# Output sums by rows of 16-token stride, without the scratch tensor for the convolution's results

## The chip, the cores and the metric

One core of one Trainium2 chip. The metric is the device time of one execution in microseconds (us), as the median of several runs. A profile is one further execution, and has a time of its own.

## The reference, cut to what matters

The kernel computes, for 2048 tokens of width 512, a gated mix of two branches:

```python
x = A_x
g = sigmoid((x * gate_w).sum(-1, keepdims=True))
a = A_ref(x, wq, wk, wv, wo, beta)   # attention
b = B_ref(x, A, B, C, log_dt, Dskip) # state-space convolution
return g * a + (1 - g) * b
```

Branch A has 32 heads of width 16 and four segments of 512 tokens. Within a segment it is causal softmax attention; each head mixes to it, by a gate of its own, a linear-attention memory of the earlier segments (elu + 1 features, M and z summed up over the segments). The heads' outputs go through `wo`. Branch B is a causal convolution of each of the 512 channels with a kernel of length 2048, `K[d, l] = Re sum_n C B dt exp(dt A l)`, plus the skip `u * Dskip`.

## The kernel before, in words

The program is a graph of 1846 steps that `build_graph` writes down (`S.op`, `S.dma`, `S.evac`); a step is one or several instructions on one engine. Which step runs when is not in the graph: the text `ORDER` (line 366) lists the numbers of all steps, and each engine executes its steps in this sequence. Behind a number, the slashes give the buffer slots that the step takes; `a` or `v` picks ACT or DVE for a copy out of PSUM that either could make. `Sched.emit` sets a semaphore wait wherever a step needs another engine's result or a buffer's last reader. An engine takes its steps strictly in this order, so a step that waits holds up those behind it on its engine. Nearly all DMAs are issued by SP, one after the other.

What the steps do:

- **x transposed** (`do_xT`, line 731) puts x into SBUF as channels by tokens (`xTT`); `gate_tokens` (903) computes the token gate g per segment, 16 matmuls of one column, an exponential on ACT (915) and small DVE operations (914 to 920). Line 918 makes 1 - g, for the output sums.
- **Attention.** For each of 4 segments s and 4 groups of 8 heads: `project` (q, k), `seg_tokens` (v), `seg_state` (the memory), `scores` (1019) in five tiles A0, B0, C, A1, B1, each with matmuls into four PSUM banks, one exponential over 2048 columns on ACT (line 1080, 80 in all), a mask (1092) and the product with V (matmuls of 17 columns); then the normalization (1052, 1053, 1055). `ophase` (1111) adds the memory and transposes the result (step oT) to channels by tokens (`oTT`).
- **Tables** (`tables`, 1148) build the convolution kernel's factors on DVE (lines 1177 to 1217).
- **Convolution** by a transform in two levels. `x_level1` (872) reads x in rows of 16-token stride (partition j holds tokens 16 j, 16 j + 1, ...) and writes the first level to the DRAM scratch `scr_Z`. `tail` (1257) runs twice, for channels 0 to 255 (half a) and 256 to 511 (half b), 16 steps each: load constants (CT, CD) and the first level (Zx) from `scr_Z`, transform (X, with two SBUF-to-SBUF moves that exchange the partition halves, also called X), the kernel's transform (K), the product (Y, line 1309), back (V, moved into V2). At its end, eight steps `fir` finish the inverse: four matmuls of 256 columns each over V2, and four of 128 columns that add the skip, whose stationary operand is `xTT` with a stride of 16 tokens, `[[16, 128]]`. A fir result has partition j holding token 16 j + b: rows of 16-token stride.
- **Bounce.** The output sums want 128 consecutive tokens on the partitions. So fir's results (`cv`) go to the scratch tensor `scr_C` by 8 DMAs and come back by 8 more (Cl) as `CTT`, tokens in sequence.
- **Output sums** (`final`, 1352; called for s and tb): for 128 consecutive tokens four matmuls of 512 columns (one for each head group) give attention times `wo` in PSUM; DVE adds (1 - g) times `CTT` (1371) and a DMA stores 128 rows to the output. For s = 3 the fourth matmul is a step of its own, behind the last transposed output. Six buffers `ou` take the results.

All matmuls are issued by the helper in line 699; copies out of PSUM by `evac` (226 on ACT, 227 on DVE); DMAs by `S.dma` (222). PSUM has 8 banks; a score tile takes four of them, always the same.

The profiles' lines name the steps by line; the names here (oT3.3 is the transposed output of segment 3, head group 3; sc, mk, pv, nrm are the tile's scores, mask, V product and normalization; Xb7 is transform step 7 of half b) are the program's tags.

## Time and profile before

| what | us |
|---|---|
| median of 3 runs | 309.71 (309.55 to 310.97) |
| the profiled execution | 306.98 |
| its span, first to last instruction | 305.2 |
| PE busy, DVE busy, ACT busy | 262.4, 269.4, 260.1 |
| time at the last exponential's start | 282.48 |
| last output sum's end | 298.9 |

A profile row gives the source line, the engine, the operation and its operands; "x16" counts instructions. "busy" is the time in which at least one of a group's instructions ran, "mean ns" that of one. In a row of the windows stand, after the stretch and its length, the busy time and count of PE, PEld (TensorE's weight loads), DVE, ACT and POOL, then the granted clock, the DMA engines' share and GB/s. In the chain of waits and in the timeline the first two numbers are start and length; a bracket tells how long the engine was idle before and what ended that. PE's busy time is longer than what its matmuls need: they are pipelined, and each has its full latency in the record.

### The profile page before, as it was taken

What the parts mean: (1) busy time and instruction counts of PE and PEld (TensorE: products, weight loads), DVE (VectorE), ACT (ScalarE), POOL (GpSimd) and SP (SyncE); (2) the same over time, 40 slices, a digit from 0 to 9 for tenths busy, and PEclk for the clock granted to TensorE, in tenths of its full rate; (3) what the DMA queues carried; (4) which work ended last, traced back from release to release, by engine and by line L of the source; (5) the groups of instructions that cost most, each with busy time, mean ns of one, the idle gap of its engine ahead of it and who ended that gap; (6) DMA issues with size and microseconds to landing.
All of it is one profiled execution on the core that took longest, in us unless ns stands there. A gap on an engine that the chain in (4) does not pass through costs nothing.

```text
span 305.2 us, 10349 instructions
## 1 busy us (share of the span) xinstructions
PE 262.4 (86%) x4360; PEld 184.8 (61%) x4395; DVE 269.4 (88%) x653; ACT 260.1 (85%) x304; POOL 7.9 (3%) x18
## 2 busy tenths in 40 slices
PE   6586678887888899999999899899899899998990
PEld 5242445653556576677766667687676777886540
DVE  2999999989999999989998987899889769989781
ACT  2999999999999999969999879899699798988200
POOL 8000000000000000000000000000000000000000
PEclk9999999999999999999999999999999999999998
DMA  7994662262234554636766466677767876367752
GB/s 172 244 232 100 146 178 77 78 100 66 85 93 110 156 163 121 193 88 176 212 176 184 145 191 196 181 220 237 232 190 218 248 227 174 97 179 217 194 174 70
DMA packets 60738, 49.89 MB, mean 163 GB/s; under 512 B 22594, under 2 KB 56019, under 8 KB 60691
## 3 DMA queue, kind: packets, MB, share of 16 engines
q1 hardware_dynamic: 59728, 48.84, 57.7%
q8 instruction: 35, 0.57, 0.9%
q0 software_dynamic: 288, 0.21, 0.5%
q10 hardware_dynamic: 674, 0.16, 0.2%
q14 instruction: 13, 0.10, 0.1%
HBM read 28.88 MB, written 8.39 MB: 122 GB/s over the span
## 4 chain that ended last, share of the span: by engine, by line
PE 32%; ACT 30%; DVE 18%; DMA 10%; issue 6%; SPq 2%; DVEq 0%; ACTq 0%
PE psum L699 31%; ACT sb L1080 17%; ACT sb L226 10%; DMA sb<-sb 4%; DMA sb<-in_A_wv_dram 3%; DVE sb L1180 3%; DVE sb L1177 2%; DVE sb L1371 2%; DVE sb L1184 2%; DVE sb L227 2%; SPq L222 2%; ACT sb L820 1%; DMA sb<-scr_Z 1%; DVE sb L1309 1%; DMA out_dram<-sb 1%
## 5 line engine op out<-in xcount | busy, mean ns | idle before, releaser
L699 PE MATMUL psum<-sb 128*128 128x17 bf16 (+12 forms) x4242 | 254.1, 224 | 29.8 <-ACT sb L1080 12.1
L699 PEld LDWEIGHTS psum<-sb 128*128 128x128 bf16 (+5 forms) x4277 | 176.5, 98 | 103.7 <-ACT sb L1080 22.2
L1080 ACT ACTIVATE sb<-psum 128x2048 bf16<-128x2048 f32 x80 | 152.2, 1902 | 9.2 <-PE psum L699 8.4
L226 ACT ACTIVATE sb<-psum 128x512 bf16<-128x512 f32 (+2 forms) x159 | 93.2, 650 | 17.4 <-PE psum L699 16.6
L227 DVE CAST sb<-psum 128x512 bf16<-128x512 f32 x62 | 42.5, 692 | 7.6 <-PE psum L699 7.4
L1309 DVE TENSOR_TENSOR sb<-sb 128x1024 bf16<-128x1024 bf16 x32 | 22.0, 686 | 5.1 <-DMA sb<-sb 4.7
L1092 DVE TENSOR_TENSOR sb<-sb 128x1024 bf16<-128x1024 bf16 (+1 forms) x40 | 22.8, 578 | 3.0 <-ACT sb L1080 2.8
L1177 DVE TENSOR_TENSOR sb<-sb 128x512 bf16<-128x512 bf16 (+4 forms) x44 | 24.5, 565 | 0.4
L1184 DVE TENSOR_TENSOR sb<-sb 128x512 bf16<-128x512 bf16 (+4 forms) x44 | 24.2, 554 | 0.5
L1180 DVE TENSOR_TENSOR sb<-sb 128x512 bf16<-128x512 bf16 (+4 forms) x44 | 24.5, 564 | 0.2
L1055 DVE TENSOR_TENSOR sb<-psum,sb 128x256 bf16<-128x256 f32 x32 | 13.5, 422 | 0.5
L820 ACT ACTIVATE sb<-sb 128x512 f32<-128x512 f32 x18 | 11.8, 655 | 0.2 <-DVE sb L802 0.2
L1371 DVE SCALAR_TENSOR_TENSOR sb<-sb,psum 128x512 bf16<-128x512 bf16 x16 | 10.7, 736 | 1.1 <-DMA out_dram<-sb 1.1
L1217 DVE TENSOR_TENSOR sb<-sb 128x2048 bf16<-128x2048 bf16 x8 | 9.6, 1224 | 0.1
L1212 DVE TENSOR_TENSOR sb<-sb 128x4096 bf16<-128x4096 bf16 x4 | 9.1, 2285 | 0.0
L1052 DVE RECIPROCAL sb<-psum 128x16 f32<-128x16 f32 x32 | 8.1, 254 | 1.1 <-PE psum L699 0.8
L1132 DVE TENSOR_TENSOR sb<-psum,sb 128x512 bf16<-128x512 f32 x12 | 8.3, 689 | 0.3
L1009 ACT ACTIVATE sb<-sb 128x512 bf16<-128x512 bf16 x12 | 7.8, 652 | 0.0
L821 DVE TENSOR_TENSOR sb<-sb 128x256 f32<-128x256 f32 x18 | 7.6, 420 | 0.2
L227 DVE COPY sb<-psum 128x1024 bf16<-128x1024 bf16 x4 | 2.8, 688 | 5.5 <-PE psum L765 5.0
L822 DVE SCALAR_TENSOR_TENSOR sb<-sb 128x256 f32<-128x256 f32 x18 | 7.6, 420 | 0.1
L958 ACT ACTIVATE sb<-psum 128x512 bf16<-128x512 bf16 x12 | 7.5, 627 | 0.1
(75 smaller groups left out, 115.8 us busy)
## 6 DMA issues: line engine op xcount, KB each, us to landing
sb<-c_DNM SPq DMA_DIRECT2D x32, 320.0 KB, 4.0
sb<-c_DNM SPq DMA_DIRECT2D x32, 192.0 KB, 3.4
sb<-sb SPq DMA_DIRECT2D x84, 64.0 KB, 2.9
scr_Z<-sb SPq DMA_DIRECT2D x16, 256.0 KB, 2.4
sb<-scr_Z SPq DMA_DIRECT2D x32, 128.0 KB, 2.8
sb<-sb SPq DMA_DIRECT2D x32, 128.0 KB
sb<-in_A_x_dram SPq DMA_DIRECT2D x5, 512.0 KB, 5.7
scr_C<-sb SPq DMA_DIRECT2D x8, 256.0 KB, 3.1
```

The source lines that it names most:

```text
L226: fa = lambda e: e.activation(dst(), src(), ACT.Copy)
L227: fd = lambda e: e.tensor_copy(dst(), src())
L699: mm = lambda e, o_, l, r_, st, sp, **kw: e.matmul(o_, lhsT=l, rhs=r_, start=st, stop=sp, skip_group_check=True, **kw)
L820: op("ACT", ("As", 512), lambda e, sq=sq, Z=Z: e.activation(ap(sq, n=512), ap(Z, n=512), ACT.Square), r=[Z], w=[sq], key=PW[h] + PWS * k)
L1055: op("DVE", ("V1", 256), lambda e: e.tensor_tensor(ap(o1, gi * 16, [[128, 4], [32, 4], [1, 16]]), ap(T, dims=[[68, 4], [17, 4], [1, 16]]), ...
L1080: o = op("ACT", ("Ax", 2048), lambda e, P=P, pT=pT: e.activation(ap(pT, n=2048), ap(P, n=2048), ACT.Exp, scale=0.25), r=[P], w=[pT])
L1092: op("DVE", ("V2", 128 * nb), lambda e, pT=pT, dims=dims: e.tensor_tensor(ap(pT, dims=dims + [[1, 128]]), ap(pT, dims=dims + [[1, 128]]), ...
L1177: op("DVE", ("V2" if n > 1 else "V1", 256 * n), lambda e: e.tensor_tensor(run(tile, ne, dst, 1), run(tile, ne, src, sstep), zz(cl * 512), ...
L1180: op("DVE", ("V2" if n > 1 else "V1", 256 * n), lambda e: e.tensor_tensor(run(t2, n, 0, 1), run(tile, ne, src, sstep), zz(cl * 512 + 256), ...
L1184: op("DVE", ("V2" if n > 1 else "V1", 256 * n), lambda e: e.tensor_tensor(D_(), D_(), ap(t2, n * 128, [[-n * 128, 2], [2 * n, 64], [1, 2 * ...
L1309: op("DVE", ("V2", 1024), lambda e, Y=Y, XAB=XAB, K3=K3: e.tensor_tensor(ap(Y, dims=[[512, 2], [1, 512]]), ap(XAB, dims=[[512, 2], [1, 512 ...
L1371: op("DVE", ("V1", 512), lambda e: e.scalar_tensor_tensor(ap(ou, n=512), ap(CTT[s], tb * 512, n=512), ap(omgT, 4 * s + tb, n=1), ap(P, n=5 ...
```

## The change

Four things, in the code:

- fir's eight results per half stay in SBUF. Eight tiles `cv` hold both halves side by side (b writes the other 256 columns). `scr_C`, its 16 DMAs and `CTT` are gone.
- `final(b)` sums the rows 16 j + b for j = 0 to 127: the stationary operand of its matmuls is `oTT` with a stride of 16 tokens, and it needs all four segments. The first three matmuls are one step and the fourth another, for all 16 sums. The store writes 128 rows that lie 16 rows apart in the output. With `CTT` gone, there are 21 buffers `ou`.
- `gate_rows` computes 1 - g once more in this row order: 64 matmuls of one column with a strided stationary operand, then clamp, exponential, add and reciprocal over 16 columns. The four products in line 918 are gone.
- `ORDER` is another list. The graph has 1843 steps; numbers shift where steps left or came.

```diff
 
 
@@ -585,7 +584,6 @@
     einvT = S.keep(64, F32)
     einvP = [einvT.part() for _ in range(4)]
     omgT = S.keep(64, F32)
-    omgP = [omgT.part() for _ in range(4)]
     gzT = S.keep(64, F32)
     gzP = [gzT.part() for _ in range(4)]
     gmaskT = S.keep(4 * 136 * 4, F32)
@@ -674,16 +672,14 @@
     YPs.append(mkpool("Yb", 2048, 3, 2))
     VPs.append(mkpool("Vb", 1024, 3, 2))
     assert a <= 207 * 1024, a - 207 * 1024
-    a = H2
-    CTT = [Tile(mkpool("C%d" % i, 4096, 1, 3), BF16) for i in range(4)]
     a = H0
     woT = Tile(mkpool("wo", 4096, 1, 3), BF16)
-    cvP = mkpool("cv", 2048, 3, 3)
-    ouP = mkpool("ou", 1024, 6, 3)
+    cvP = mkpool("cv", 2048, 8, 3)
     assert a <= H2, a - H2
+    ouP = mkpool("ou", 1024, (T0 - a) // 1024, 3)
+    assert a <= T0, a - T0
 
     Zd = nc.dram_tensor("scr_Z", (32 * 128 * 512,), BF16)
-    Cd = nc.dram_tensor("scr_C", (2048 * 512,), BF16)
 
     class DT:
         def __init__(self):
@@ -866,8 +862,7 @@
                r=[ident, dcolT], pw=[diagT])
 
     dZ = DT()
-    dC = [DT() for _ in range(2)]
-    Cp = {(s, h): CTT[s].part() for s in range(4) for h in range(2)}
+    cvs = {}
 
     def x_level1():
         for qd in range(4):
@@ -915,10 +910,26 @@
         op("ACT", ("Asx", 4), lambda e: e.activation(g(expT), g(gzT), ACT.Exp, scale=-1.0), r=[gzP[s]], w=[expP[s]])
         op("DVE", ("V1", 4), lambda e: e.tensor_scalar_add(g(einvT), g(expT), 1.0), r=[expP[s]], w=[einvP[s]])
         op("DVE", ("R", 4), lambda e: e.reciprocal(g(gzT), g(einvT)), r=[einvP[s]], w=[gzP[s]])
-        op("DVE", ("V1", 4), lambda e: e.tensor_tensor(g(omgT), g(expT), g(gzT), ALU.mult), r=[expP[s], gzP[s]], w=[omgP[s]])
+        S.tag = "gateo%d" % s
         oms[s] = Tile(omsP, F32)
         op("DVE", ("V1", 128), lambda e: e.tensor_tensor(ap(oms[s], dims=[[32, 4], [1, 32]]), ap(omghT, dims=[[0, 4], [1, 32]]),
                                                          ap(gzT, 4 * s, [[1, 4], [0, 32]]), ALU.mult), r=[omghT, gzP[s]], w=[oms[s]])
+
+    def gate_rows():
+        S.tag = "gater"
+        P = S.ps()
+
+        def f(e):
+            for b in range(16):
+                for k in range(4):
+                    i = mm(e, ap(P, b, n=1), ap(xTT[0], k * 2048 + b, [[16, 128]]), ap(gwT, k, n=1), k == 0, k == 3)
+            return i
+        op("PE", c_pe("F", *[1] * 64), f, r=xTT + [gwT], w=[P])
+        w = lambda: ap(omgT, n=16)
+        op("DVE", ("V1", 16), lambda e: e.tensor_scalar(w(), ap(P, n=16), -60.0, 60.0, ALU.max, ALU.min), r=[P], w=[omgT])
+        op("ACT", ("Asx", 16), lambda e: e.activation(w(), w(), ACT.Exp), w=[omgT])
+        op("DVE", ("V1", 16), lambda e: e.tensor_scalar_add(w(), w(), 1.0), w=[omgT])
+        op("DVE", ("R", 16), lambda e: e.reciprocal(w(), w()), w=[omgT])
 
     vpad = {}
     states = {}
@@ -1322,55 +1333,46 @@
             S.evac(lambda V=V: ap(V, n=512), lambda PI=PI: ap(PI, n=512), 512, r=[PI], pw=[V])
             S.dma(lambda t=t: ap(V2, 0, [[512, 16], [1, 512]], p0=v2_row(t), np_=8, pstep=4),
                   lambda V=V: ap(V, n=512), 131072, r=[V], pw=[V2])
-        for g4 in range(4):
-            S.key = k0 + 10 + dk * 16 + 2 * g4
-            cv = Tile(cvP, BF16)
-            for b2 in range(2):
-                S.tag = "fir%s%d" % (hn, 2 * g4 + b2)
-                P = S.ps()
-
-                def f2(e, P=P, b0=4 * g4 + 2 * b2):
-                    for j in range(2):
-                        for kt in range(2):
-                            i = mm(e, ap(P, j * 256, n=256), ap(G2T, kt * 128, n=128), ap(V2, ((b0 + j) * 2 + kt) * 256, n=256),
-                                   j == 0 and kt == 0, False)
-                    for j in range(2):
-                        for kk in range(2):
-                            k = 2 * half + kk
-                            i = mm(e, ap(P, j * 256 + kk * 128, n=128), ap(xTT[0], k * 2048 + b0 + j, [[16, 128]]), ap(diagT, k * 128, n=128),
-                                   False, j == 1 and kk == 1)
-                    return i
-                op("PE", c_pe("F", *[256] * 4 + [128] * 4), f2, r=[G2T, V2, diagT] + xTT, w=[P], acq=[cv])
-                S.evac(lambda cv=cv, b2=b2: ap(cv, b2 * 512, n=512), lambda P=P: ap(P, n=512), 512, r=[P], pw=[cv])
-            S.dma(lambda g4=g4: bass.AP(Cd, g4 * 2048 + half * 256, [[8192, 128], [512, 4], [1, 256]]),
-                  lambda cv=cv: ap(cv, dims=[[256, 4], [1, 256]]), 262144, r=[cv], pw=[dC[half]])
-        for s in range(4):
-            S.tag = "Cl%s%d" % (hn, s)
-            S.dma(lambda s=s: ap(CTT[s], half * 256, [[512, 4], [1, 256]]),
-                  lambda s=s: bass.AP(Cd, s * 262144 + half * 256, [[512, 128], [65536, 4], [1, 256]]), 262144, r=[dC[half]], pw=[Cp[(s, half)]])
-
-    def final(s, tb):
-        S.tag = "fin%d.%d" % (s, tb)
+        for g2 in range(8):
+            S.key = k0 + 10 + dk * 16 + g2
+            if half == 0:
+                cvs[g2] = Tile(cvP, BF16)
+            cv = cvs[g2]
+            S.tag = "fir%s%d" % (hn, g2)
+            P = S.ps()
+
+            def f2(e, P=P, b0=2 * g2):
+                for j in range(2):
+                    for kt in range(2):
+                        i = mm(e, ap(P, j * 256, n=256), ap(G2T, kt * 128, n=128), ap(V2, ((b0 + j) * 2 + kt) * 256, n=256),
+                               j == 0 and kt == 0, False)
+                for j in range(2):
+                    for kk in range(2):
+                        k = 2 * half + kk
+                        i = mm(e, ap(P, j * 256 + kk * 128, n=128), ap(xTT[0], k * 2048 + b0 + j, [[16, 128]]), ap(diagT, k * 128, n=128),
+                               False, j == 1 and kk == 1)
+                return i
+            op("PE", c_pe("F", *[256] * 4 + [128] * 4), f2, r=[G2T, V2, diagT] + xTT, w=[P], acq=[cv])
+            S.evac(lambda cv=cv: ap(cv, half * 256, [[512, 2], [1, 256]]), lambda P=P: ap(P, dims=[[256, 2], [1, 256]]), 512, r=[P], pw=[cv])
+
+    def final(b):
+        S.tag = "fin%d.%d" % (b // 4, b % 4)
         P = S.ps()
-        t0 = 512 * s + 128 * tb
         ou = Tile(ouP, BF16)
-
-        def att(e, hg, last):
-            return mm(e, ap(P, n=512), ap(oTT[0], hg * 2048 + t0, n=128), ap(woT, hg * 512, n=512), hg == 0, last)
-
-        nh = 3 if s == 3 else 4
+        cv = cvs[b // 2]
+
+        def att(e, hg):
+            return mm(e, ap(P, n=512), ap(oTT[0], hg * 2048 + b, [[16, 128]]), ap(woT, hg * 512, n=512), hg == 0, hg == 3)
 
         def f(e):
-            for hg in range(nh):
-                i = att(e, hg, hg == 3)
+            for hg in range(3):
+                i = att(e, hg)
             return i
-        o = op("PE", c_pe("F", *[512] * nh), f, r=[woT] + [oTp[(s, hg)] for hg in range(nh)], w=[P], acq=[ou])
-        if s == 3:
-            o.deps.append(last_score[0])
-            op("PE", c_pe("F", 512), lambda e: att(e, 3, True), r=[woT, oTp[(s, 3)]], pw=[P])
-        op("DVE", ("V1", 512), lambda e: e.scalar_tensor_tensor(ap(ou, n=512), ap(CTT[s], tb * 512, n=512), ap(omgT, 4 * s + tb, n=1),
-                                                                ap(P, n=512), ALU.mult, ALU.add), r=[P, omgP[s], Cp[(s, 0)], Cp[(s, 1)]], w=[ou])
-        S.dma(lambda: bass.AP(out, t0 * 512, [[512, 128], [1, 512]]), lambda: ap(ou, n=512), 131072, r=[ou])
+        op("PE", c_pe("F", *[512] * 3), f, r=[woT] + [oTp[(s, hg)] for s in range(4) for hg in range(3)], w=[P], acq=[ou])
+        op("PE", c_pe("F", 512), lambda e: att(e, 3), r=[woT] + [oTp[(s, 3)] for s in range(4)], pw=[P])
+        op("DVE", ("V1", 512), lambda e: e.scalar_tensor_tensor(ap(ou, n=512), ap(cv, (b % 2) * 512, n=512), ap(omgT, b, n=1),
+                                                                ap(P, n=512), ALU.mult, ALU.add), r=[P, omgT, cv], w=[ou])
+        S.dma(lambda: bass.AP(out, b * 512, [[8192, 128], [1, 512]]), lambda: ap(ou, n=512), 131072, r=[ou])
 
     S.key = 0.0
     pb, dt, Zs = ssm_prep()
@@ -1401,6 +1403,8 @@
             scores(s, hg, TA0 + GA * i0)
             S.key = TA0 + GA * (i0 + 7.5)
             ophase(s, hg)
+    S.key = TA0 + GA * 40
+    gate_rows()
     for c in range(4):
         S.key = TT0 + TT * c
         tables(c)
@@ -1408,9 +1412,8 @@
     x_level1()
     tail(0, TK0, TDK)
     tail(1, TK0 + 60.0, TDK)
-    for s in range(4):
-        for tb in range(4):
-            final(s, tb)
+    for b in range(16):
+        final(b)
     return S
```

The two lists, each a text of its own, begin and end so:

```diff
 ORDER = """
-13/0 8/0 10/0 11/4 12/1 0/0 28/4/0 18/0 29v 34/5 26/0 195/0 196 197 35/0 44/0 6/0 9/0 45/1 1246/0 60/1 1262/0/0 1263a
...
-1842/1/2 1817 1804 1806/2/4 1807 1838/3/5 1839 1805 1840 1843 1834/4/3 1808 1835 1841 1844 1845 1836 1830/5/1 1831
-1837 1832 1833
...
+1834 1812 1819/5/8 1813 1814 1805 1806 1820 1791/6/9 1821 1822 1792 1815/0/10 1793 1816 1823/1/11 1824 1794 1807/2/12
+1808 1825 1826 1835/3/13 1836 1817 1818 1809 1810 1787/4/14 1837 1838 1788 1779/0/15 1780 1789 1790 1781 1782
 """
```

What stands in them, by the steps' tags (a step that both graphs have is shared):

| | before | after |
|---|---|---|
| steps on PE, ACT, DVE, SP | 570, 304, 653, 305 | 583, 307, 650, 289 |
| sequence of the 80 exponentials | | the same |
| shared PE steps at another place | | 363 of 550, by 1.5 places on average |
| shared DVE steps at another place | | 532 of 604, by 7.0 on average |
| PSUM copies on ACT, of the 265 free to move that are shared | 165 | 167 |
| the 64 matmuls of gate_rows on PE | | behind the scores sc1.1.B0, ahead of Ka1 |
| load Zxb0 on SP | behind Xa14's two moves, CDb0, Va12's store | ahead of CTb0, both moves of Xa14, Va12's store |
| SP entries between the two moves of one X, half a, in all | 8 | 15 |
| the same, half b, in all (largest) | 32 (6) | 76 (16) |
| output steps on PE ahead of the last score tile's V product (pv3.3.B1, second part) | 6 | 3, with three matmuls each |
| output sums on DVE ahead of the last normalization | 3 | 0 |
| oT3.3 on PE | behind ten output steps | behind five |

More of the change, by code (lines that the diff above doesn't have):

```diff
@@ L457 @@
[L457 to L458 removed]
+8/0 10/4 18/0 12/0 11/4 0/0 13/1 1247/0 6/0 34/4 35/0 28/0/0 29v 37/0 38/1 44/2 9/1 26/0 36/3 45/4 60/1 1265/0/0
+1253/1/1 43/5 39/6 46/7 40 195/0 47 1266a 3/0 41 48 42 50/8 51/9 15/2 14/3 23/0 196 25/0 49 1255/4 1256a 63/5 64v/0
+16/4 52/10 54/0 56/11 1/0 61/6 62v 1263/0 1264a 53 55/12 65/0 57/13 1254a 197 67/1 30/5/1 31v 66 68v/0 80v/1 77/1 17/5
+79/2 78 220/4/0 221a 216/0 217a 69 202/2 198/0 91/3 32/1/2 179/4 21/0 89/2 90 33a 59/0 208/3/0/0 209v 19/0 7/0 103/5
@@ new lines @@
+1692/2/2 1698/1 1701/4/3 1702a 1674/0 1675/5/2 1676a 871/3/2/0 1651 925/1 1652 1655/2 1691 1712/0 1619 844 1693v
+1694/1 1739/2 884/1 1656/0/0 1737/4 813/4 1434 1657a 814a 1671 1705/5/1 872 873 883 914/0/3/1 845/2 1706a 1750/0
+1738/1 874 1752/1 859/0/2 860 1678 1725/2 1677 926 915 916 917 1726/0 848 1718/3/2 1719a 853 965 1645 1703 1740/0/1
+1695/1/1 1741v 1743 1696a 1697 849 850 854 855/4 856 906/0/3 907 1753/3/0 1754v 1755 1724/3 861 1742 1545/0/0 1713/2
+857/0 1546v 1543/1/1 1544a 1547/3/2 858/2 1704 1681/0 885/0/1 862 1548v 1682/0/2 1711/2 1744/1/0 1745v 1756 886 887
```

169 lines of the change are left out of this document (80 added, 89 removed).

## The prediction

> **What bounds the kernel now.** I read the page first, for how loaded the engines are and who owns the chain that ended last; then the windows, to split the span into a long middle and an end; then the timeline of the end, because that is the stage which the change rebuilds.
>
> ```profile
> span 305.2 us, 10349 instructions
> PE 262.4 (86%) x4360; PEld 184.8 (61%) x4395; DVE 269.4 (88%) x653; ACT 260.1 (85%) x304; POOL 7.9 (3%) x18
> ...
> PE 32%; ACT 30%; DVE 18%; DMA 10%; issue 6%; SPq 2%; DVEq 0%; ACTq 0%
> ```
>
> ```profile
> 25.00:284.40 259.40, 233.06 (x4133) 168.57 (x4156) 238.42 (x579) 240.79 (x272) 1.30 (x2) 1.00 0.58 162
> 284.40:299.00 14.60, 12.75 (x105) 6.48 (x103) 12.81 (x23) 0.60 (x1) 0.00 (x0) 1.00 0.53 165
> ```
>
> The columns after the length are PE, PEld, DVE, ACT and POOL busy. No engine is the bound by itself: from 25 to 284.4 us ACT is idle for 259.40 - 240.79 = 18.6 us and DVE for 259.40 - 238.42 = 21.0 us, and the chain hops between PE, ACT and DVE. The granted clock is 1.00 in both stretches, so it plays no part. The end is different: ACT is done and DVE and PE do the output sums.
>
> ```profile
> 282.48 1.88 ACT L1080 ACTIVATE sb<-psum 128x2048 bf16<-128x2048 f32 x1 [0.55 <-PE psum L699]
> 284.39 0.69 DVE L1092 TENSOR_TENSOR sb<-sb 128x1024 bf16<-128x1024 bf16 x1 [1.65 <-ACT sb L1080]
> 285.17 1.97 DVE L1371 SCALAR_TENSOR_TENSOR sb<-sb,psum 128x512 bf16<-128x512 bf16 x3
> 288.21 0.26 DVE L1052 RECIPROCAL sb<-psum 128x16 f32<-128x16 f32 x1 [0.52 <-PE psum L699]
> 288.72 0.42 DVE L1055 TENSOR_TENSOR sb<-psum,sb 128x256 bf16<-128x256 f32 x1
> 289.09 5.36 DVE L1371 SCALAR_TENSOR_TENSOR sb<-sb,psum 128x512 bf16<-128x512 bf16 x8
> 292.13 0.60 ACT L226 ACTIVATE sb<-psum 128x512 bf16<-128x512 f32 x1 [7.77 <-PE psum L699]
> 295.52 3.38 DVE L1371 SCALAR_TENSOR_TENSOR sb<-sb,psum 128x512 bf16<-128x512 bf16 x5 [1.07 <-DMA out_dram<-sb]
> ```
>
> The last exponential ends at 282.48 + 1.88 = 284.36. Its mask, its product with V and its normalization end at 288.72 + 0.42 = 289.14; three of the sixteen output sums (L1371) run ahead of that normalization, thirteen after it. The last sum ends at 295.52 + 3.38 = 298.90. The remaining 305.2 - 298.9 = 6.3 us are the last store and the waits of SP, which I take as unchanged.
>
> **The change part by part.**
>
> *The scratch bounce goes.*
>
> ```profile
> scr_C<-sb SPq DMA_DIRECT2D x8, 256.0 KB, 3.1
> sb<-scr_C SPq DMA_DIRECT2D x8, 256.0 KB, 3.9
> out_dram<-sb SPq DMA_DIRECT2D x16, 128.0 KB, 1.7
> ```
>
> ```profile
> L222 SPq DMA_DIRECT2D scr_C<-sb x8: 359/363/495, 249.3 to 276.8; - x8
> L222 SPq DMA_DIRECT2D sb<-scr_C x8: 360/508/544, 277.2 to 288.0; - x8
> ```
>
> Sixteen DMAs of 256 KB leave SP's queue. The loads of the second half start at 277.2, eight microseconds ahead of the first sum, and no sum waits for one: the only DMA wait in the end stage is the 1.07 us for an output buffer. So the bounce is hidden, by the last softmax tiles, and its removal is worth 0. It can't shorten earlier loads either, since its first store is issued at 249.3.
>
> *The sums move behind all attention.* A row of 16-token stride has tokens of all four segments, so the fourth matmul of every sum needs the last transposed output (oT3.3). All sixteen sums of DVE now stand behind it, where before only thirteen stood behind the normalization, which comes earlier still. I follow the new end with these prices:
>
> ```profile
> L699 PE MATMUL psum<-sb 128*128 128x17 bf16 x28 | 0.8, 170 | 0.0
> ```
>
> ```profile
> L699 PE MATMUL psum<-sb 128*128 128x128 bf16 x4 | 0.4, 226 | 0.0
> ```
>
> ```profile
> L699 PE MATMUL psum<-sb 128*128 128x512 bf16 x11 | 2.5, 379 | 0.0
> ```
>
> A matmul's spacing is the group's busy time less the last one's own duration, over the steps: (0.8 - 0.17) / 27 = 0.023 us for 17 columns, (0.4 - 0.226) / 3 = 0.058 for 128, (2.5 - 0.379) / 10 = 0.21 for 512. DVE's sums come every (5.36 - 0.74) / 7 = 0.66 us (the five at the end: (3.38 - 0.74) / 4 = 0.66; one by itself takes 0.74, the mean of the row below). Hand-overs cost about 0.05 each.
>
> ```profile
> L1371 DVE SCALAR_TENSOR_TENSOR sb<-sb,psum 128x512 bf16<-128x512 bf16 x16 | 10.7, 736 | 1.1 <-DMA out_dram<-sb 1.1
> ```
>
> The mask ends at 284.39 + 0.69 = 285.08. The last sixteen 17-column matmuls: 0.05 + 15 x 0.023 + 0.17, to 285.65. Normalization, as before from 288.21 to 289.14, 0.93: with its hand-over, to 286.6. In the old order DVE's three early sums and PE's output matmuls stood here; that they go is worth 289.14 - 286.6 = 2.5 us. Then the transposes (eight of 128 columns, 0.05 + 7 x 0.058 + 0.23, to 287.3), ACT's copy (0.05 + 0.60, to 287.95), the first fourth matmul (0.05 + 0.38, to 288.4), and sixteen sums: 15 x 0.66 + 0.74 = 10.6, to 299.1. Before: 298.9. **Term: +0.2.** The 1.07 us for an output buffer is not in it, as there are now 21 buffers where there were six.
>
> The cover of this is PE: 7 sums have three of their four matmuls done by then, so 7 + 9 x 4 = 43 are left, 43 x 0.21 = 9.0 us from 288.0, to 297.0; DVE starts its last sum at 299.1 - 0.74 = 298.4. PE has 1.4 us to spare.
>
> *Weights in strides.* The output matmuls and the new gates read their stationary operand 32 bytes apart. The convolution's last matmuls (fir) do so already:
>
> ```profile
> L699 PEld LDWEIGHTS psum<-sb 128*128 128x128 bf16 x4 | 0.4, 147 | 0.0
> ```
>
> ```profile
> L699 PEld LDWEIGHTS psum<-sb 128*128 128x128 bf16 x61 | 4.9, 97 | 5.0
> ```
>
> The first row is four strided loads in fir, 147 ns; the second the loads of the present output stage, 97 ns. Those 61 loads hide behind matmuls 0.21 apart, and 0.147 still fits into 0.21. Term 0 for the sums. The Trainium skill, in "TensorE: Matmul & The Clock Gate", section "The mechanism", says that a weight load overlaps a running matmul only where their row groups differ; these all use the full array, so by it nothing would hide. The trace disagrees for loads of 97 ns; for strided loads under 512 columns no row shows it, and that is a rival below.
>
> *The new gates (gate_rows).* 64 matmuls of one column, each with a strided load of its own. Bounds: 64 x 0.023 = 1.5 us (as dense as the 17-column ones) and 64 x 0.1 = 6.4 (four loads in 0.4 us). I take the spacing of the strided 128-column matmuls, the nearest row: 64 x 0.058 = 3.7 us of PE. They stand between the exponentials of the second segment, where PE already makes the path:
>
> ```profile
> 112.97 2.13 PE psum L699 x60
> 115.10 0.07 issue
> 115.17 2.23 PE psum L699 x15
> ```
>
> ```profile
> 100.00:112.00 12.00, 10.74 (x183) 7.21 (x177) 11.51 (x38) 11.95 (x14) 0.00 (x0) 1.00 0.48 133
> ```
>
> PE is idle for 1.3 us of the 12 before, so they aren't free. But PE holds only 32% of the chain over the span, and a delay in one engine's stretch is partly absorbed where another bounds. I charge that share: 0.32 x 3.7 = **+1.2** (ends 0 and 6.4).
>
> *Small operations and who evacuates.*
>
> ```profile
> L914 DVE TENSOR_SCALAR sb<-psum 128x4 f32<-128x4 f32 x4 | 0.6, 156 | 0.0
> ...
> L918 DVE TENSOR_TENSOR sb<-sb 128x4 f32<-128x4 f32 x4 | 0.6, 156 | 0.0
> ```
>
> ```profile
> L917 DVE RECIPROCAL sb<-sb 128x4 f32<-128x4 f32 x4 | 0.7, 177 | 0.0
> L916 DVE TENSOR_SCALAR sb<-sb 128x4 f32<-128x4 f32 x4 | 0.7, 163 | 0.0
> ```
>
> ```profile
> L227 DVE CAST sb<-psum 128x512 bf16<-128x512 f32 x62 | 42.5, 692 | 7.6 <-PE psum L699 7.4
> L226 ACT ACTIVATE sb<-psum 128x512 bf16<-128x512 f32 (+2 forms) x159 | 93.2, 650 | 17.4 <-PE psum L699 16.6
> ```
>
> DVE loses four L918 and two evacuations and gains three operations of the gates: -4 x 0.156 - 2 x 0.692 + 0.156 + 0.163 + 0.177 = -1.5 us. ACT gains the two evacuations and one small exponential, 2 x 0.65 + 0.2 = +1.5. By their shares of the chain: -1.5 x 0.18 + 1.5 x 0.30 = **+0.2**.
>
> *The order.* The exponentials keep theirs, all 80; 363 of PE's 550 shared steps move, by 1.5 places on average. One place can be read off. The load of the second half's first transform (Zxb0, 1564 in the old list, 1557 in the new) is on the chain:
>
> ```profile
> 187.78 1.25 SPq L222 DMA_DIRECT2D sb<-sb x2
> 189.08 0.45 SPq L222 DMA_DIRECT2D sb<-scr_Z  x1
> ```
>
> ```profile
> 189.08 3.81 DMA sb<-scr_Z
> ```
>
> ```profile
> PEld psum L699 <- DMA sb<-scr_Z: 1.3, 1, 1.3
> ```
>
> SP issues it at 189.08, behind Va12's store and the moves of Xa14. In the new list it stands ahead of those, and of CTb0. The 3.81 us go; the load path waited 1.3 of them, and behind it PE is late anyway. **Term: -1.3.** Against that, the two moves that make up an exchange (Xb) stood at most 6 SP entries apart, 32 in all, and now up to 16, 76 in all. For the rest of the new order I find no row with a sign: I take 0, with ends of a quarter of DVE's 21.0 us idle time either way, -5 and +5.
>
> *Output rows.* Each store writes 128 rows of 1 KB, now 16 KB apart. The scratch stores have that distance with 512-byte pieces: 3.1 us for 256 KB, against 1.7 for an output store. Only the last store counts: 0, at most 3.1 - 1.7 = +1.4.
>
> **Sum:** +0.2 + 1.2 + 0.2 - 1.3 = +0.3. The profiled execution took 306.98 us and lies 2.73 below the median of the runs, 309.71; so 307.3 for a profile, 310.0 for the median. What a measurement of this kernel can tell from no change is about 0.5%, 1.55 us.
>
> **The rivals.**
> 1. *The new order packs the middle better.* For it: 21.0 us of DVE and 18.6 of ACT idle in the middle, much of it behind waits of one step. Against: same exponentials, small moves, and wider Xb pairs. A quarter of DVE's idle time: 309.7 - 5.2 = 304.5.
> 2. *The gates hit PE whole.* Slower. In 112 to 118 the chain is nearly all PE, so 3.7 us in front delay the exponentials behind them; it decides where the steps behind them wait for PE alone, and not for ACT or DVE. 3.7 in place of 1.2: 312.5.
> 3. *The exchanges come late.* The multiplication behind an exchange already waits for it at times:
>
> ```profile
> L1309 DVE TENSOR_TENSOR sb<-sb 128x1024 bf16<-128x1024 bf16 x32 | 22.0, 686 | 5.1 <-DMA sb<-sb 4.7
> ```
>
> A pair 10 SP entries apart, at some 0.5 us each (0.45 and 1.25 / 2 in the rows of SP above), lands 5 us late; it decides if the multiplication behind it was due within that time. One such wait, as long as the load's 3.81: 310.0 + 3.8 = 313.8.
> 4. *Strided loads don't hide.* 43 x (0.21 + 0.147) = 15.4 us of PE in place of 9.0 with 1.4 to spare: +5.0, 315.0.
>
> That the change doesn't do what it says is in the forecast: the bounce goes, and nothing had waited for it.
>
> **How the numbers follow.** Forecast (no difference that shows, own range 308.2 to 311.5): 0.35, of which 0.05 faster, 0.25 within 0.5%, 0.05 slower. Rival 1: 0.32, faster. Rival 2: 0.14; rival 3: 0.13; rival 4: 0.04, all slower. Left over 0.02, within. So faster 0.37, same 0.27, slower 0.36. The range takes in rivals 1 to 4 and the ends of the order's term: 304.0 to 315.0.
>
> **What would show it.** The scratch tensor is gone from the DMA rows and nothing else in the end moves earlier for it. Right: the last exponential ends within 1.5 us of 284.4; the normalization follows it by 2.3 us, the sixteen sums run with no gap 4 us behind it at 0.66 us, and the last ends 14.8 behind it. Wrong: output matmuls more than 0.24 us apart with DVE waiting for PE (rival 4); a gap between exponentials around 108 to 120 us longer by over 2 us (rival 2); the Xb multiplications (L1309) waiting more than 4.7 us in all for DMA (rival 3); DVE's idle time in the middle under 17 us (rival 1).

## The result and the profile after

| | before | after |
|---|---|---|
| median, us (all executions of the comparison) | 309.63 (306.33 to 311.39) | 315.59 (310.80 to 317.86) |
| profiled execution; its span | 306.98; 305.2 | 316.78; 315.0 |
| end of the last exponential | 284.36 | 293.98 |
| end of the last output sum | 298.90 | 309.32 |

After to before is 1.0124, with a 95% interval of 1.0084 to 1.0165: slower, where I forecast no difference that shows. This ratio leaves out the executions in a slower state, to which the profiled ones of after, e1 and e9 to e12 belong and that of before does not, and the medians hold all, which is why 315.59 / 309.63 is 1.019 and the two profiles lie 9.8 us apart. So the profiles below show where time went in two single executions, and not how the 1.2% divides. By the ratio the time is 1.0124 x 309.71 = 313.6 us, inside the range of 304.0 to 315.0; the median of all lies 0.6 above its end.

The head of the page of after, its instruction queues and its chain:

```profile
span 315.0 us, 10488 instructions
PE 275.4 (87%) x4459; PEld 193.6 (61%) x4459; DVE 268.7 (85%) x650; ACT 260.2 (83%) x307; POOL 8.3 (3%) x18
...
q8 instruction: 35, 0.57, 0.8%
...
PE 40%; ACT 28%; DVE 14%; DMA 7%; issue 7%; SPq 3%; ACTq 0%; DVEq 0%
```

DVE and ACT do the work they did (269.4 and 260.1 before). PE is busy for 13 us more and holds 40% of the chain instead of 32%. The row q8 will matter: 35 packets and 0.57 MB of instructions, 16 KB each.

The windows show that the end is not where the time went (columns as before):

```profile
25.00:294.00 269.00, 244.31 (x4218) 173.66 (x4219) 239.22 (x578) 242.55 (x277) 1.31 (x2) 0.98 0.52 144
294.00:309.30 15.30, 13.84 (x112) 9.33 (x110) 12.84 (x23) 0.60 (x1) 0.00 (x0) 1.00 0.36 121
```

The middle is 269.0 us where it was 259.4, and its mean granted clock is 0.98 where it was 1.00. From the end of the last exponential to the end of the span: 315.0 - 293.98 = 21.0 us, before 305.2 - 284.36 = 20.8. The forecast had +0.2 for this. The timeline of the end, ACT and DVE:

```profile
292.10 1.88 ACT L1091 ACTIVATE sb<-psum 128x2048 bf16<-128x2048 f32 x1 [0.51 <-PE psum L695]
295.96 0.42 DVE L1066 TENSOR_TENSOR sb<-psum,sb 128x256 bf16<-128x256 f32 x1
297.18 0.60 ACT L226 ACTIVATE sb<-psum 128x512 bf16<-128x512 f32 x1 [3.20 <-PE psum L695]
298.70 10.62 DVE L1373 SCALAR_TENSOR_TENSOR sb<-sb,psum 128x512 bf16<-128x512 bf16 x16 [2.31 <-PE psum L695]
```

Three places of the middle carry most of what the profiles differ by. The first is the stretch of the gates. In the timeline of ACT, the exponential ahead of them and the one behind:

```profile
108.89 1.87 ACT L1091 ACTIVATE sb<-psum 128x2048 bf16<-128x2048 f32 x1
...
115.77 1.88 ACT L1091 ACTIVATE sb<-psum 128x2048 bf16<-128x2048 f32 x1 [0.59 <-PE psum L695]
```

They start 6.9 us apart; in the timeline of before the same two are these, 3.3 apart:

```profile
107.69 1.88 ACT L1080 ACTIVATE sb<-psum 128x2048 bf16<-128x2048 f32 x1
...
110.99 1.92 ACT L1080 ACTIVATE sb<-psum 128x2048 bf16<-128x2048 f32 x1
```

In between PE runs the 64 new matmuls (groups of 108.2 to 112.25 us), and then 3.4 us at a granted clock of 0.50 (windows, the number ahead of the last two):

```profile
L695 PE MATMUL psum<-sb 128*128 128x1 bf16 x64 | 4.1, 200 | 0.0
```

```profile
108.60:112.00 3.40, 3.40 (x59) 3.40 (x58) 2.60 (x5) 3.17 (x4) 0.00 (x0) 1.00 0.34 78
112.00:115.40 3.40, 3.40 (x26) 1.96 (x25) 0.50 (x3) 0.73 (x1) 0.00 (x0) 0.50 0.02 5
```

In the first of these windows PE does nothing but matmuls of one column, in the next it has half the clock. The Trainium skill, "TensorE: Matmul & The Clock Gate", section "What's actually happening", says that the gate judges PE's activity in free-running windows of about 3.4 us and halves the clock after an idle one. The length agrees with this trace. If that rule is what acts here, 3.4 us of one-column matmuls count for little activity, although PE's busy time is the full 3.40; e2 below puts this to the test.

The second place is two stops of PE at 141 and 186 us, of which the first is shown here (chain of waits; a shorter one, 1.15 us at 102.7, stands ahead of the gates):

```profile
140.49 0.22 PE psum L966 x4
140.71 0.43 PE psum L695 x26
141.14 2.00 issue
143.14 1.12 PE psum L695 x15
```

"issue" means that PE waits for nothing that the profile shows, in the midst of a run of equal matmuls. The third is a load from scr_Z behind the second stop: SP has its entries queued up until 195, and issues this load last.

```profile
186.15 1.74 issue
...
194.41 0.67 SPq L222
195.13 6.16 DMA sb<-scr_Z
```

### The profile page after: what moved, and what is told of

Same layout as the page of the kernel before. It is cut to its first block, busy times and chain, and to the rows that moved or that the text cites. A ratio compares the mean times of both kernels' runs of the same rounds, so it can differ in the third digit from the quotient of the medians.

```text
span 315.0 us, 10488 instructions
## 1 busy us (share of the span) xinstructions
PE 275.4 (87%) x4459; PEld 193.6 (61%) x4459; DVE 268.7 (85%) x650; ACT 260.2 (83%) x307; POOL 8.3 (3%) x18
## 4 chain that ended last, share of the span: by engine, by line
PE 40%; ACT 28%; DVE 14%; DMA 7%; issue 7%; SPq 3%; ACTq 0%; DVEq 0%
PE psum L695 39%; ACT sb L1091 15%; ACT sb L226 8%; DVE sb L1373 3%; DMA sb<-sb 3%; SPq L222 3%; ACT sb L816 2%; DMA sb<-scr_Z 2%; DMA sb<-in_B_A_im_dram 2%; DVE sb L227 2%; DVE sb L1195 1%; DVE sb L1191 1%; DVE sb L1320 1%; ACT sb L969 1%; DVE sb L1228 1%
## 5 line engine op out<-in xcount | busy, mean ns | idle before, releaser
L695 PE MATMUL psum<-sb 128*128 128x17 bf16 (+15 forms) x4341 | 266.9, 226 | 26.5 <-ACT sb L1091 12.9
L695 PEld LDWEIGHTS psum<-sb 128*128 128x128 bf16 (+5 forms) x4341 | 184.4, 100 | 104.6 <-ACT sb L1091 23.9
L226 ACT ACTIVATE sb<-psum 128x512 bf16<-128x512 f32 (+3 forms) x157 | 91.7, 645 | 18.4 <-PE psum L695 17.9
L227 DVE CAST sb<-psum 128x512 bf16<-128x512 f32 (+1 forms) x64 | 43.4, 689 | 14.0 <-PE psum L695 13.7
```

The costliest lines, as they stand in the source:

```text
L226: fa = lambda e: e.activation(dst(), src(), ACT.Copy)
L227: fd = lambda e: e.tensor_copy(dst(), src())
L695: mm = lambda e, o_, l, r_, st, sp, **kw: e.matmul(o_, lhsT=l, rhs=r_, start=st, stop=sp, skip_group_check=True, **kw)
```

## The experiments

Each expectation names its theories for itself. The medians are beside those of the kernel before in the same comparison; ratios are to before.

**e1_few_gates.** Four gate matmuls in place of 64 (one gate row in sixteen is made):

```diff
-            for b in range(16):
-                for k in range(4):
-                    i = mm(e, ap(P, b, n=1), ap(xTT[0], k * 2048 + b, [[16, 128]]), ap(gwT, k, n=1), k == 0, k == 3)
+            for k in range(4):
+                i = mm(e, ap(P, n=16), ap(xTT[0], k * 2048, [[16, 128]]), ap(gwT, k, [[0, 16]]), k == 0, k == 3)
```

> The changed kernel with 4 matmuls of 16 columns in place of gate_rows' 64 of one column; the gates of 15 of every 16 rows are left out (all rows of a partition take the gate of the first). Theory G (the gates cost it: some 3.7 us of TensorE, and a window of 3.41 us at half clock that follows because the array does next to nothing meanwhile): 3.5 to 6 us less than the changed kernel, about the kernel before (within 0.5%), and no half-clock window at 108 to 116 us. Theory O (the new order costs it): no more than 1.5 us less, so still about 1% over the kernel before.

Measured 308.09 us beside 308.46, ratio 0.998 (0.9932 to 1.0028). Without the 64 matmuls nothing is lost: new order, new end and strided sums together cost nothing that shows. One sign of theory G failed: e1's profile, too, has 3.4 us at a granted clock of 0.50, from 114.0 us, behind 3.4 us in which PE was busy for 1.6. So a half-clock window at this place is not proof of the gates.

**e2_wide_gates.** The 64 gate matmuls stream 96 columns each, of which the last written one counts.

```diff
-                    i = mm(e, ap(P, b, n=1), ..., ap(gwT, k, n=1), k == 0, k == 3)
+                    i = mm(e, ap(P, b, n=96), ..., ap(gwT, k, [[0, 96]]), k == 0, k == 3)
```

> The changed kernel with the same 64 strided weight loads in gate_rows, but 96 columns streamed behind each (the next gate's column overwrites the surplus), which fits under the 0.06 us that a strided load takes: same time on TensorE, but the array busy for two thirds of it. If the half clock is what the gates cost (theory G, second half): no half-clock window after it, 1.5 to 3 us less than the changed kernel. If it is the 3.7 us of loads themselves: same time as the changed kernel, within 1 us. Theory O: the same.

Measured 314.70 beside 308.46, 1.0227 (1.0163 to 1.029). Their spacing is the same, 64 in 4.1 us, and no half-clock window follows them in the profile (the granted clock is 1.00 from 108 to 116 us). In after, e4 and e11, where 3.4 us were filled with such matmuls of one column, 3.4 us at 0.50 followed each time. Yet e2 is no faster than after, so the loss as a whole does not hang on the half clock behind the gates. Its profile also parts the gates' own time from the half clock. The exponential ahead of the gates and the one behind:

```profile
109.11 1.87 ACT L1091 ACTIVATE sb<-psum 128x2048 bf16<-128x2048 f32 x1
```

```profile
114.57 1.88 ACT L1091 ACTIVATE sb<-psum 128x2048 bf16<-128x2048 f32 x1
```

They start 5.46 us apart, 2.2 more than in before, where after's are 3.6 further apart. So of 4.1 us of gates 2.2 delay the exponentials, and the other 1.4 go with the half clock; this is an estimate from single profiles.

**e3_before_gates.** The kernel before with `gate_rows` added at the same place, its result unused.

```diff
+    op("PE", c_pe("F", *[1] * 64), fg, r=xTT + [gwT], w=[PG])
+    ...
+    op("DVE", ("R", 16), lambda e: e.reciprocal(wg(), wg()), w=[growT])
```

> The kernel before with gate_rows added at the same neighbours of its order; its result is not used, all else is unchanged. Theory G: 3.5 to 6 us over the kernel before, and a half-clock window behind it. Theory O: at most 1.5 us over.

Measured 313.59 beside 308.46, 1.019 (1.0131 to 1.0249). The gates alone, in the old graph and order, bring as much as the whole change.

**e4_old_order.** The kernel after with its steps in the sequence of before as far as scores tile C of segment 3, head group 3, then as in after. Only `ORDER` differs; its head:

```diff
-8/0 10/4 18/0 12/0 11/4 0/0 13/1 1247/0
+13/0 8/0 10/0 11/4 12/1 0/0 28/4/0 18/0
```

> The graph of the changed kernel in the old order: shared steps as in the list of before, on the same engines, gate_rows at the same neighbours, and from the scores of sc3.3.C on the list of the changed kernel. Theory G: as slow as the changed kernel, or within 1.5 us of it (the order carries nothing). Theory O: at least 2.5 us faster than the changed kernel, and within 0.5% of the kernel before plus what the end costs (0.8 us by the profiles).

Measured 316.52 beside 308.46, 1.0299 (1.0232 to 1.0366). The old order is not faster. It isn't a clean test, as its end is longer too: 17.35 us from the last exponential to the last sum, where after has 15.34.

**e5_unit_stride.** The gate matmuls read their weights with unit stride (the gates are then those of other tokens).

```diff
-ap(xTT[0], k * 2048 + b, [[16, 128]])
+ap(xTT[0], k * 2048 + b * 128, n=128)
```

> The changed kernel with gate_rows' weights read with unit stride (128 tokens in sequence: the gates come out in the wrong rows). If the stride is what makes the 64 loads dear: they take 64 x 0.025 = 1.6 us in place of 4.05, and the kernel gets 2 to 3.5 us shorter, about 0.5 to 1% over the kernel before. If the number of instructions or the place counts and not the stride: unchanged, 1.2 to 2% over.

Measured 313.09 beside 309.69, 1.0149 (1.0091 to 1.0207). The group of gates in its stretch:

```profile
L695 PE MATMUL psum<-sb 128*128 128x1 bf16 x64 | 1.7, 163 | 0.0
```

1.7 us instead of 4.1, and the loss stays. At this place the gates now cost nothing, for the exponentials around them start 3.34 us apart, where before has 3.30:

```profile
107.89 1.87 ACT L1091 ACTIVATE sb<-psum 128x2048 bf16<-128x2048 f32 x1
```

```profile
111.23 1.89 ACT L1091 ACTIVATE sb<-psum 128x2048 bf16<-128x2048 f32 x1
```

So e5 loses its time elsewhere. What e2, e3 and e5 have in common with after is the number of PE's instructions, and PE's waits show it. Rows of the waits of PE for before, after, e1, e2, e3 and e5 in this order (us in total, times, longest):

```profile
PE psum L699 <- issue: 3.0, 7, 1.3
```

```profile
PE psum L695 <- issue: 4.9, 3, 2.0
```

```profile
PE psum L695 <- issue: 1.1, 6, 0.3
```

```profile
PE psum L695 <- issue: 5.0, 10, 1.7
```

```profile
PE psum L699 <- issue: 4.8, 10, 2.3
```

```profile
PE psum L695 <- issue: 4.6, 9, 1.9
```

Before has 3.0 us of its own, so after's are 1.9 more; the kernel that stands out is e1, with after's graph and 1.1.

**e6_gates_moved.** The five steps of `gate_rows` stand later in `ORDER`, just ahead of transform step 2 of half b (the first of them, by its neighbours):

```diff
-1136 1006/3 1149
+1136 1149
...
-1583/0 1584/3/1
+1583/0 1006/2 1584/3/1
```

> The changed kernel with the 64 gate matmuls moved from behind sc1.1.B0 to just ahead of the transform Xb2, where TensorE of the changed kernel waits 2.6 us for a DMA; all else as changed. If the cost is TensorE time on the path at that place (theory: 4 us where TensorE is the bound): 2 to 4 us less, as the wait hides them. If the cost is the sum of TensorE's time over the kernel: within 1 us of the changed kernel.

Measured 313.95 beside 309.69, 1.0182 (1.0108 to 1.0255). Here the issue waits are small (1.2 us, the longest 0.2) and the loss stays. Its expectation of 2 to 4 us less failed: at the new place the exponentials ahead of the gates and behind them start 14.0 us apart (193.14 and 207.15), 7.0 more than in before, and 6.8 us at half the clock, from 198.1, are in it. So there are two causes, not one: the gates' work costs without such stops, too.

**e7_gates_dma and e8_gates_dma_tail.** No gate matmuls: 1 - g is made in token order, and two GpSimd DMAs bring it into rows over DRAM, in pieces of 4 bytes. e8 also moves the second pair of output matmuls that stands ahead of the first sum behind the first eight sums.

```diff
+        S.dma(lambda: bass.AP(Gd, 0, [[1, 128], [128, 16]]), lambda: ap(growT, n=16), 8192, r=[growT], w=[dG], slow=True, q="POOL")
+        S.dma(lambda: ap(omgT, n=16), lambda: bass.AP(Gd, 0, [[16, 128], [1, 16]]), 8192, r=[dG], w=[omgT], q="POOL")
```

> The changed kernel with 1 - g brought into row order by a bounce of 8 KB through DRAM (two DMAs issued by GpSimd, one DVE operation) in place of gate_rows; everything computed. If the gates on TensorE are the whole loss: as with the few gates, within 0.5% of the kernel before, 4 to 6 us under the changed kernel. If something else of the change costs as well: 0.5 to 1% over the kernel before.

> As the run before, and the three matmuls of one output sum (fin1.2) that stand between the last transposes and the first fourth matmul go behind the first eight sums. If TensorE's order there delays the first sum: it starts 0.6 to 0.7 us earlier after the last exponential, and the sums end 14.7 us behind it in place of 15.3. If DVE's order or the copy is what it waits for: no change.

Measured 318.01 and 316.58 beside 309.69, 1.0259 (1.0169 to 1.0348) and 1.0283 (1.0198 to 1.0369): a miss, by a new cause. Up to the DMA e7 is as before: the 57th exponential starts at 212.55 us in before, at 224.54 in after and here at 213.30 (timelines of ACT). At 211.53 GpSimd issues the first of the two DMAs, the store; the load follows only at 229.91, when the store has landed. The windows of e7 from 205 us on:

```profile
205.00:211.60 6.60, 6.55 (x95) 5.08 (x94) 5.56 (x12) 6.54 (x7) 0.07 (x1) 1.00 0.68 197
211.60:221.50 9.90, 7.22 (x124) 5.54 (x122) 7.41 (x18) 7.53 (x9) 1.11 (x1) 1.00 0.93 66
221.50:235.20 13.70, 5.28 (x48) 2.98 (x50) 1.82 (x5) 2.99 (x3) 1.20 (x2) 0.50 0.74 168
```

The DMA engines are busy for 0.93 of the time and move a third of what they did (66 GB/s after 197), PE waits up to 8.4 us for a load from scr_Z, and runs the next 13.7 us at half the clock. In e8, with the store issued at 211.62, they are busy for 0.64 of the same 9.9 us and move 62 GB/s, and PE waits up to 6.8 us. So the store of 8 KB, by its place in both traces, costs about 10 us; that its 4-byte pieces are the reason was not tried alone. The end of e8 gains less than expected: its first sum starts 4.3 us behind the last exponential and its last sum ends 14.97 behind, where e7 has 4.7 and 15.35.

**e9_few_padded, e10_before_padded, e11_after_padded.** The test of the code. Unread matmuls of one column go into the second warm-up group, where PE waits for the first loads; 60 for e1, 64 for before and after.

```diff
-    for _ in range(3):
+    for w_ in range(3):
         PW_ = S.ps()
-        def fw(e, PW_=PW_):
+        def fw(e, PW_=PW_, w_=w_):
+            for j in range(60 if w_ == 1 else 0):
+                i = e.matmul(ap(PW_, j % 4, n=1), lhsT=ap(oneT, n=128), rhs=ap(oneT, n=1), start=True, stop=True, skip_group_check=True)
```

> The kernel after with the four 16-column gate matmuls of the kernel e1_few_gates (15 of 16 gate rows are left out) and, in the second warm-up group at the start, where PE waits 3.5 us for the first loads, 60 matmuls of one column whose result nothing reads. PE has as many instructions as in the kernel after, and no gate work. Theory A (the 128 further instructions shift the borders of the 16 KB pieces in which PE's code arrives, and PE then stands at borders): PE's waits put down to issue at 4 to 5 us, as after (4.9), 312 to 315 us, ratio 1.010 to 1.020. Theory B (the gate matmuls' own time and the half clock behind them): as without them, 308 us, ratio 0.995 to 1.003, issue near 1 us.

> The kernel before, with 64 matmuls of one column whose result nothing reads in the second warm-up group at the start, where PE waits 1.6 us. Nothing else differs but the borders of the pieces of PE's code behind it, by half a piece. Theory A: slower, 311 to 314 us, ratio 1.007 to 1.015, issue waits above the 3.0 us of before. Theory B: at most 0.5 us for the start, ratio 0.998 to 1.003.

> The kernel after with 64 unread matmuls of one column in the second warm-up group: ahead of the gates the code now stands half a piece further than in e1_few_gates, and behind them a whole piece, so that the borders lie where e1_few_gates has them. Theory A: issue waits behind the gates fall from 4.9 to 1 to 2 us, and the time to 309 to 311 us, ratio 0.999 to 1.006. Theory B: as after, 313 to 315 us, ratio 1.010 to 1.017.

Measured, all beside 308.46: e9 312.26, 1.0132 (1.0079 to 1.0185), as theory A had it. e10 307.21, 0.9962 (0.9911 to 1.0013), against A's slower. e11 310.88, 1.0102 (1.0053 to 1.015), the time that A had, with a ratio above A's and inside B's.

e9 has no gate work, and loses as much as after. The 60 unread matmuls themselves cost nothing at their place: the first exponential starts at 23.1 us in e9, e1 and after alike. Its chain of waits shows a stop at the same instruction as after's at 141.14: four matmuls of line 967 (966 in after), 26 small ones, and then nothing.

```profile
136.34 0.22 PE psum L967 x4
136.56 0.43 PE psum L697 x26
136.99 1.72 issue
138.71 1.88 PE psum L697 x22
```

Counted through the records, with weight loads and semaphore instructions, three stops of over 0.6 us in each of the two kernels stand at PE's instructions 3009, 4289 and 5825. All three are 193 above a multiple of 256. (A fourth wait of e9, 1.5 us at 254.9, is put down to issue as well, but stands at a semaphore.) The 0.57 MB of the row q8 in 35 packets are 16 KB each, 64 bytes for each of 256 instructions. So each stop is at the same place within such a piece of code: PE has used one up and the next isn't there. In after the packet's record starts at 140.7 us, takes 0.9, and PE goes on at 143.14. It is alike at all six stops: PE goes on 1.3 to 1.6 us after the end of a packet's record. Why it matters where a border lies shows the timeline of PE in after:

```profile
137.91 2.58 PE L695 MATMUL psum<-sb 128*64 128x40 bf16 x132
140.32 0.39 PE L966 MATMUL psum<-sb 128*128 128x128 bf16 x4
140.64 0.50 PE L695 MATMUL psum<-sb 128*32 128x40 bf16 x26
143.14 2.89 PE L695 MATMUL psum<-sb 128*32 128x40 bf16 x66 [2.00 <-issue]
```

Here 132 small matmuls, each with a weight load, are 264 instructions in 2.58 us: a whole piece is gone in about the time from the packet's start to PE's next matmul, 2.4 us. The 256 instructions ahead of the three stops ran in 3.6, 2.4 and 3.1 us in after and in 2.9, 2.4 and 3.1 in e9. (One more piece of after is as short, 3.1 us, and ends in no stop.) In e11 the borders lie elsewhere in the program: every piece takes 3.9 us or more but one of 2.9, which ends in a stop of 0.1, and the same stretch, row by row, has no stop:

```profile
136.09 1.70 PE L697 MATMUL psum<-sb 128*64 128x40 bf16 x96 [0.22 <-DVE sb L1197]
137.72 0.40 PE L968 MATMUL psum<-sb 128*128 128x128 bf16 x4
137.96 4.61 PE L697 MATMUL psum<-sb 128*128 128x512 bf16 x148
142.41 0.39 PE L968 MATMUL psum<-sb 128*128 128x128 bf16 x4
142.73 2.19 PE L697 MATMUL psum<-sb 128*32 128x40 bf16 x58
```

e11 has no issue wait among PE's groups at all, where after has 4.9 us. Yet its profiled execution, 316.48 us, is as long as after's 316.78: it spends 20.4 us at half the clock ahead of its end, after 10.2 and before none. So this profile shows that the stops go, and only the ratio can tell what that gains. The Trainium skill, "Runtime: NRT & Kernel Launch", section "Instruction fetch mechanics", has the blocks of 16 KiB and 256 instructions, which these runs show, and says that crossing a border is mostly hidden. For runs of small matmuls they show otherwise: 0.8 to 2.0 us each in after and e9. A stop can cost more than its length: 6.8 us at half the clock follow the one near 137 us in e9 and in e5 (from 139.5 and from 139.0).

e10 is the limit of this theory: the kernel before has stops of its own (3.0 us, the longest 1.3 at 63.2), the shift removes that one and brings others (2.5 us in all, the longest 0.9), and no time is lost. Its two longest stand in runs of 40-column matmuls, too, again 193 above a multiple of 256. So a border in such a run brings a stop, but not every stop lengthens the kernel; what decides that was not tried.

**e12_select_tail.** 1 - g in rows from the gates that exist: a mask spreads them, one float matmul of 16 columns picks. The second pair of output matmuls goes behind the first eight sums.

```diff
+        op("DVE", ("V1", 128), lambda e: e.tensor_tensor(ap(selT, dims=[[8, 16], [1, 8]]), ap(gzT, dims=[[1, 16], [0, 8]]),
+                                                         ap(bdT, dims=[[0, 16], [17, 8]]), ALU.mult), r=gzP + [bdT], w=[selT])
+        op("PE", c_pe("F", 64), lambda e: mm(e, ap(P, n=16), ap(selT, n=128), ap(modT, n=16), True, True), r=[selT, modT], w=[P])
+        op("DVE", ("V1", 16), lambda e: e.tensor_scalar(ap(omgT, n=16), ap(P, n=16), -1.0, 1.0, ALU.mult, ALU.add), r=[P], w=[omgT])
```

> The kernel after with its 16-stride gate rows made from the gates that are there already: one DVE multiplication spreads the 16 columns of gates over 128 under a mask, one float matmul of 16 columns picks the rows, one DVE operation makes 1 - g. The 64 gate matmuls, the exponential and the reciprocal go; a constant of 8 KB is loaded at the start. And the second pair of projection matmuls that stands ahead of the first output sum is moved behind the first eight sums. Both theories: no gate work and no further code, so as e1_few_gates without its sum's wait: 307 to 308 us, ratio 0.990 to 0.999; last sum 14.7 to 15.0 us behind the start of the last exponential, where after has 15.34. If the 128 instructions and the gate work are not what costs (theory C, the new order costs by itself), 312 to 314.

Measured 308.18 beside 308.46, 0.9993 (0.9965 to 1.0022): the loss is gone, which speaks against theory C, but it does not beat before; 0.990 to 0.999 was expected. Its last sum ends 14.96 us behind the last exponential (15.34 in after). At the start it lost what it gained: PE waits longer for a load that every later step needs (waits of PE, e1 then e12).

```profile
PE psum L761 <- DMA sb<-in_B_A_im_dram: 3.5, 1, 3.5
```

```profile
PE psum L764 <- DMA sb<-in_B_A_im_dram: 4.9, 1, 4.9
```

The only DMA added there is the constant that the picking matmul reads (modT), 8 KB in pieces of 64 bytes. That it is the reason was argued, not tried.

**What the runs say together.** Ratios to before, each within its own comparison:

| | code borders as in e1 | code borders as in after |
|---|---|---|
| no gate work | e1: 0.998 | e9: 1.013 |
| 64 gate matmuls | e11: 1.010 | after: 1.012 |

Against e1 the borders alone (e9) cost 1.5% and the gates alone (e11) 1.2%, and neither interval meets that of e1 (0.9932 to 1.0028). e5 agrees on the borders: its gates delay no exponential, its longest stop is 1.9 us, and it stands at 1.0149. So that each of the two causes costs is shown. That they add up is not: after, which has both, stands no higher than e9 or e11 alone, and taking its stops away (e11) gains nothing that the intervals tell apart. How much of the 1.2% belongs to which stays open.

## Why the prediction was right and wrong, point by point

The 313.6 us lie inside the range, 304.0 to 315.0, but outside the forecast's own, 308.2 to 311.5, and slower had 0.36 of the chances. That the range held is in part luck: its upper end came from rival 4, which was wrong, and the second cause, the stops, stood in no term and no rival.

- *The bounce hides: right.* The scr_C rows are gone, and e1, which has all of the change but the gates, stands at 0.998.
- *The end, +0.2: right as a sum,* 21.0 after 20.8. Inside it the first sum starts 298.70 - 293.98 = 4.7 us behind the last exponential, not 4.0: DVE waited 2.31 us for PE, since I let the first sum's fourth matmul follow ACT's copy at once, and the order puts other sums' matmuls ahead of it. e12 has 0.4 of this back. And 5.7 us follow the last sum, not 6.3.
- *Strided weights hide under 512 columns (rival 4 wrong): right.* In the stretch of the sums 42 output matmuls take 9.3 us, (9.3 - 0.38) / 41 = 0.22 apart, and DVE's 16 sums run without a gap.

```profile
L695 PE MATMUL psum<-sb 128*128 128x512 bf16 x42 | 9.3, 380 | 0.0
```

- *Exchanges late (rival 3): no.* Line 1309, now 1320, waits 2.5 us for DMA, where it waited 4.7.

```profile
L1320 DVE TENSOR_TENSOR sb<-sb 128x1024 bf16<-128x1024 bf16 x32 | 21.7, 683 | 5.4 <-ACT sb L226 2.8 <-DMA sb<-sb 2.5
```

- *The gates, "I charge that share: 0.32 x 3.7 = +1.2": the step that failed.* The price was right, 0.062 us apiece where I took 0.058. The charge was wrong: the exponentials behind the gates come 3.6 us further apart, and rival 2's sign (over 2 us) is there. By e2 about 2.2 of this is the gates' own time, more than half of their 4.1 and not a third; the other 1.4 go with the half clock, so that rival 2's 3.7 was met in part by luck. A share of the chain over the whole span says little of a stretch in which the chain, by my own row, was nearly all PE. Nor is all of it the rule: e5's 1.7 us of gates cost nothing there. And the term had no place for what 128 more instructions do to the code behind them: the stops at 103, 141 and 186 us hold PE for 1.15 + 2.00 + 1.74 us, all 4.9 of its issue waits, where before has 3.0 in shorter ones. e9 shows that they come without any gate work.
- *The order, Zxb0 -1.3: wrong.* PE waited 2.6 us for scr_Z in after and 1.0 in before. Zxb0 was no longer late, but another load of that queue was, behind the second stop. e1, with the same order and no stops, has no such wait, nor has e11; e9, with the stops, has 1.7. But e1 waits 2.6 us for a move from SBUF to SBUF instead. The order itself I took as 0, and e1 gives no sign against that.
- *Packing (rival 1): no.* DVE is idle for 269.00 - 239.22 = 29.8 us of the middle, where it was 21.0 and the sign was under 17.
- *Small operations, +0.2: not settled.* DVE's busy time fell by 0.7 us, not 1.5, and ACT's rose by 0.1, not 1.5; no run prices them alone.
- *The half clock* was in no term: "The granted clock is 1.00 in both stretches, so it plays no part" holds for before's profile alone. After's has three such windows ahead of its end, from 71.0, 112.0 and 200.7 us, and e1, e10 and e12, which lose nothing, have them in their profiles as well.

## What to carry to other kernels

Charge PE work by the slack of its own stretch, not by PE's share of the span: here 1.7 us of it cost nothing and 4.1 us cost 2.2. Count instructions as well as time: a block of many tiny matmuls shifts the code behind it, and a run of small matmuls can stop where a border of the code falls into it; a few unread matmuls in idle time at the start test that. When a value exists already in another order, look for one matmul that rearranges it before computing it again in 64.

## What the runs showed of the hardware

- PE's code arrives in pieces of 16 KB; a run of 40-column matmuls uses one up in 2.5 us, and PE then stood for 0.8 to 2.0 us, at instruction 193 of a piece each time in after and e9, and went on 1.3 to 1.6 us after a packet's record ended.
- A one-column matmul whose weights lie 32 bytes apart comes every 0.062 us, with unit stride every 0.025 (in e5 the last of the 64 starts 1.58 us after the first).
- 3.4 us filled with one-column matmuls were followed by 3.4 us at half the granted clock in after, e4 and e11; the same number with 96 columns (e2) were not.
- While one store of 8 KB in 4-byte pieces was under way, the DMA engines moved 66 GB/s (e7, 93% busy) and 62 GB/s (e8, 64% busy) for 9.9 us, where they had moved 197.
